# Expert order computed inside the first half of expert 0; three weights of expert 1 loaded and two split there; an own buffer for the places

## The chip, the core and the metric

The kernel runs on one core of a Trainium2 chip. Its time is the device time of one execution in microseconds (us), taken as the median of several executions; lower is better. TensorE (PE in the profile) has a granted clock with two levels, 1.2 and 2.4 GHz, which the profile writes as 0.50 and 1.00.

## The reference, cut to what matters

Three stages follow one another. Shapes: 4 batches, 8 heads, 768 positions, head size 48, so 3072 tokens of 384 values.

```python
for t in range(S):                                   # 1. linear attention with a decay
    state = alpha[:, :, t, :, None] * state + k_t v_t^T
    y[:, :, t] = q_t @ state
expert_idx = argmax(xn @ en.T / tau)                 # 2. each token goes to one of 8 experts
for e in range(8):
    out[mask_e] = gate_w[mask_e] * (relu(x[mask_e] @ w1[e]) @ w2[e])
for e in range(4):                                   # 3. every token through 4 experts
    out += p[:, e:e+1] * (relu(x @ w1[e]) @ w2[e])
```

Every expert has w1 of 384 x 1024 and w2 of 1024 x 384.

## The kernel before, in words

Stage 1 walks over 24 units of 128 tokens (loop `for i in range(NU + 5)` in `attention_and_routing`); unit u passes through `S1`, `S2` and `S3` in three successive rounds. Routing runs behind it in six groups of units: `route_a` picks each token's expert, `rank` counts the place within it on TensorE, `route_b` and `route_c` make the gate, `scale` applies it, and `scatter` writes the token's row (tile `xb`) with an indirect DMA of GpSimd into the region of its expert in `xs` in HBM.

Stage 2 runs the experts in the order of their number of tokens, expert 0 first and the others by falling count. Its windows have 448, 448, 432 ... 384 columns (`WIN`). Products are split for precision: each float32 operand becomes a rounded high part and a rest, and every product takes three matmuls. `h_split` cuts a hidden block so: ScalarE writes the high part `hh` with Relu, VectorE the rest `hl`. A weight unit (128 x 768, 384 KB; eight to an expert, units 0 to 7 are expert 0's, 8 to 15 those of the next) is loaded by `load_w` through SP's queue into one of 3 buffers `wraw`, and split by `split_w` into one of 10 buffers `wu`: ScalarE copies the high part (L74), GpSimd subtracts (L75).

The first 224 columns of expert 0 (`EARLY`) are done while stage 1 ends: `early_load` reads their rows, `early_rows` turns them over on TensorE and cuts them, `early_g1(f)` is the first product of block f, `early_relu(b)` cuts blocks 2b and 2b+1 (its rest, the "rest" of the change's name, is a VectorE instruction), `early_g2(f)` the second product. The function `tail` sets their order. At its end, between `early_g1(7)` and `early_g2(4)`, the matmul `pc` adds up the tokens of each expert. VectorE then computes from `pc` the order of the experts `ordi` (L938 to L945), the columns `offi`, and through the tile `pv` the place of each token, `posi` (L948 to L963).

Then `experts` starts. `window(e)` loads the rows of an expert with SP's queue (L173) into one of two buffers `xw`; for expert 0 these are the remaining 224 columns, in three pieces. `place(e)` (L203) reads `ordi` into an SP register, which the loads of expert 1 and later, rows and weights, have in their addresses. `xpose(e)` turns a window over on TensorE, and ScalarE (L197) and VectorE (L198) cut it; `columns` writes finished columns into `x2` (L218, L219). The loop over e and f issues for each block first product, `h_split`, and the second product `g2` of the block before. `xpose(1)` is spread over blocks 3 and 4 of expert 0 and the start of expert 1.

Every engine, SP's queue too, works in the order in which the program issues: the instruction order is written out by hand, and a wait of one instruction holds all behind it on its engine. The buffers of stage 2 lie in memory that the pools of stage 1 gave back; the first writer of such a buffer waits for the last reader of what lay there.

Of the kernel before, what the change touches and what calls it, by code (L numbers as in the profile page):

```python
# [20 lines left out]
NFB = FF // 128  # L21
# [92 lines left out]
def experts(ctx, tc, a, keep, small, xs, info_d, scat, wtile, ids, load_w, split_w, out, banks, psA, ps1):  # L114
# [8 lines left out]
    def h_split(ps, n):  # L123
        hh = hp.tile([128, 512], F32R, tag="hh", name="hh")
        hl = hp.tile([128, 512], F32R, tag="hl", name="hl")
        nc.scalar.activation(out=hh[:, 0:n], in_=ps, func=AF.Relu)  # L126
        nc.vector.scalar_tensor_tensor(  # L127
            out=hl[:, 0:n], in0=ps, scalar=0.0, in1=hh[:, 0:n].bitcast(F32), op0=ALU.max, op1=ALU.subtract
        )
        return hh, hl  # L130
# [23 lines left out]
    with ExitStack() as c1:  # L154
# [52 lines left out]

        window(0)
        place(1)
        load_w(NFB + 1)  # L210
        window(1)
        regs = {}
        xpose(0)
        pos, hs = {}, {}
# [25 lines left out]
        for e in range(E1):  # L240
            if e == 1:

                xpose(1, [2])
                g2(*prev)
                prev = None
                banks.close()
                psx = c1.enter_context(tc.tile_pool(name="psx", bufs=2, space=PSUM, reuse_waits="tile"))
                psh = c1.enter_context(tc.tile_pool(name="psh", bufs=3, space=PSUM, reuse_waits="tile"))
                pso = c1.enter_context(tc.tile_pool(name="pso", bufs=1, space=PSUM, reuse_waits="tile"))
                bank["h"] = lambda: psh.tile([128, W0], F32, tag="h", name="h")  # L250
                bank["xt"] = lambda e, k: psx.tile([128, W0], F32, tag="xt", name="xt")
                bank["o"] = lambda d: pso.tile([128, W0], F32, tag=f"o{d}", name=f"o{d}")
            for f in range(NFB):
                if e or f > 1:
                    split_w(e * NFB + f + 9)
                if f == 1 and e + 2 < E1:
                    place(e + 2)
                    window(e + 2)
                n = SIZE[e]
                ps = bank["h"]()[:, 0:n]  # L260
                xh, xl = xts[e]
                gemm1(ps, wtile[e * NFB + f], lambda k: xh[:, k, 0:n], lambda k: xl[:, k, 0:n])
                hs[e, f] = h_split(ps, n)
                if prev:
                    g2(*prev)
                prev = (e, f)
                if 3 <= f < (6 if e else 5) and e + 1 < E1:
                    xpose(e + 1, [f - 3])
                if e == 1 and f == 2:
                    pfl = bank["h"]()[0:1, 0:1]  # L270
                    nc.tensor.matmul(pfl, lhsT=keep["ft"][:, 0:1], rhs=keep["ones"][:, 0:1], start=True, stop=True)
                    nc.vector.tensor_copy(keep["flag"], pfl)
                if e and f == 2:
                    regs[e] = column(nc.scalar, e), column(nc.vector, e)
                if f % 2 and 4 <= e * 4 + f // 2 < 28:
                    info(e * 4 + f // 2 - 4)
            if e == E1 - 1:
                ins = nc.sync.dma_start(out=infc, in_=info_d.rearrange("(t p) c -> p t c", p=128))
                after(ins, infs, "all rows")
                nc.vector.tensor_scalar(toki, infc[:, :, 4], float(NT - 1), 0.0, op0=ALU.min, op1=ALU.max)  # L280
# [58 lines left out]
def attention_and_routing(tc, a, small, keep, xs, info_d, wst, wtile, load_w, split_w, psA, ps1):  # L339
# [5 lines left out]
    with ExitStack() as ctx:  # L345
# [464 lines left out]

        def tail(hl0):
            hl0()
            hl1 = early_relu(1)
            hl1()
            early_g2(0)
            early_g2(1)
            early_g1(4)
            early_g1(5)
            hl2 = early_relu(2)
            hl2()  # L820
            early_g2(2)
            early_g2(3)
            early_g1(6)
            early_g1(7)
            hl3 = early_relu(3)
            hl3()
            pc = er["pc"] = mk("pc", 128, 8)
            nc.tensor.matmul(pc, lhsT=oneb, rhs=cum, start=True, stop=True)
            for f in range(4, NFB):
                early_g2(f)  # L830

        for i in range(NU + 5):
            for g in range(2, NG):
                if max(0, 3 * g - 8) == i:
                    load_in(g, 0)
                if max(0, 3 * g - 6) == i:
                    load_in(g, 1)
            for g in range(1, NG):
                if 3 * g - 2 == i:
                    load_v(g)  # L840
            if 0 < i <= E1:
                prefill(i - 1)
            if 5 <= i < 27 and i % 2:
                load_w(min((i - 3) // 2, NFB))

            steps = []
            for g in range(1, NG):
                for pp in range(2):
                    at = 3 * g - 4 + pp - (g > 2)
                    if g == 1 and pp == i:  # L850
                        steps.append((2, lambda g=g, pp=pp: prep1(g, pp)))
                    if g > 1 and at + 1 == i:
                        steps.append((0, lambda g=g, pp=pp: prep1(g, pp, part=1)))
                    if g > 1 and at == i:
                        steps.append((1, lambda g=g, pp=pp: prep1(g, pp, part=0)))
            steps = [f for _, f in sorted(steps, key=lambda x: x[0])]
            if steps and i > 1:
                steps.pop(0)()
            if 0 < i < NU:
                S1(i)  # L860
            if i == 1:
                prep_emb3()
            if 0 <= i - 2 < NU:
                S3(i - 2)
            for r, (u0, u1) in enumerate(groups):
                if i == u1 + 2 and r < last:
                    rank(r)
            if 0 <= i - 1 < NU:
                S2(i - 1)
            for r, (u0, u1) in enumerate(groups):  # L870
                if i == u1 + (3 if r < last else 2) and r <= last:
                    route_b(r)
                if i == u1 + 1:
                    flush(sums)
                    if r > last:
                        early_g1(0)
                    route_a(r)
                    if r >= last:
                        rank(r)
                    if r > last:  # L880
                        early_g1(1)
                        hl0 = early_relu(0)
                        early_g1(2)
                        early_g1(3)
            for f in steps:
                f()
            for g in range(1, NG):
                for pp in range(2):
                    at = 3 * g - 3 + pp - (g > 2)
                    if at == i:  # L890
                        prep2(g, pp, nc.gpsimd, nc.gpsimd)
                    if at + 1 == i:
                        prep4(g, pp)
            if i == 0:
                fill()
            if i == 2:
                prep_info()
            for r, (u0, u1) in enumerate(groups):
                if i == u1 + 1 and r > last:
                    route_b(r)  # L900
                if i == u1 + (4 if r < last else 2 if r == last else 1):
                    route_c(r)
                    scale(r)
                    if r < last:
                        scatter(r)
                    if r > last:
                        scatter(last)
                        scatter(r)
                        count(r)
                        tail(hl0)  # L910
            if 6 <= i < 22 and i % 2 == 0:
                split_w((i - 4) // 2)
            flush(late)
            flush(sums)
            if i == EARLY_U + 5:
                early_load()
            if i == NU:
                early_rows()
        cnt, key, num, srt, offc = (
            c1.tile([128, 8], F32, name=n) for n in ("cnt", "keys", "num", "srt", "offc")  # L920
        )
# [22 lines left out]
        dot(srt, sel, iot)  # L944
        nc.vector.tensor_scalar(keep["ordi"], srt, float(E1 - 1), 0.0, op0=ALU.min, op1=ALU.max)  # L945

        dot(srt, sel, cnt)
        nc.vector.tensor_tensor(out=num, in0=srt, in1=wins, op=ALU.min)  # L948
        nc.vector.tensor_tensor_scan(offc[:, 1:8], ones[:, 1:8], num[:, 0:7], 0.0, op0=ALU.mult, op1=ALU.add)
# [3 lines left out]

        dot(off, gt3, cnt)
        nc.vector.tensor_tensor(out=off, in0=off, in1=loff[:, 1, :], op=ALU.subtract)
        pv = wk.tile([128, NU, 8], F32, tag="At", name="pv")
        nc.vector.tensor_tensor(
            out=pv, in0=ohb, in1=off.unsqueeze(1).to_broadcast([128, NU, 8]), op=ALU.mult
        )
# [1 line left out]
        nc.vector.tensor_reduce(out=pf, in_=pv, op=ALU.add, axis=AX.X)  # L961
        nc.vector.tensor_tensor(out=pf, in0=pf, in1=slotf, op=ALU.add)
        nc.vector.tensor_scalar(keep["posi"], pf, float(NT - 1), 0.0, op0=ALU.min, op1=ALU.max)  # L963

        ft = keep["ft"]
        nc.vector.tensor_reduce(out=ft[0:R, 0:1], in_=aacc, op=ALU.max, axis=AX.XY)
# [330 lines left out]
```

## Time and profile before

| | |
|---|---|
| time, median of 3 runs | 1237.86 us (1236.94 to 1239.62) |
| time of the profiled execution | 1224.77 us |
| its span, first to last instruction | 1222.9 us |
| mean granted TensorE clock | 0.982 |
| busy: PE, PEld, DVE, ACT, POOL | 1179.8, 1082.2, 394.3, 331.3, 306.6 us |
| HBM traffic | 64 GB/s over the span |

PE is TensorE's matmuls, PEld its weight loads, DVE VectorE, ACT ScalarE, POOL GpSimd, SP the engine that issues most loads. The times of the views below are us from the span's start. Stage 1 lies at 0 to about 159 us, the early half of expert 0 at 159 to 181, its other half at 181 to 212, the other experts of stage 2 until about 400, stage 3 after that.

### The profile page before, as it was taken

How to read it: one execution, taken by the hardware profiler on the slowest of the kernel's cores; microseconds unless marked ns; L12 is line 12 of the kernel's file. 1: busy time of each engine (PE TensorE's matmuls, PEld its weight loads, DVE VectorE, ACT ScalarE, POOL GpSimd, SP SyncE). 2: the span in 40 equal slices, each digit the busy share in tenths (PEclk: the TensorE clock that was granted, in tenths of full speed). 3: DMA queues.
4: the chain of work that ended last, by engine and by line, in shares of the span. 5: the costliest groups of instructions: out<-in, count | busy, mean ns of one | idle time of the engine just before them, and what ended most of it. 6: DMA issues, size and time to landing. Idle time of an engine off the chain costs nothing.

```text
span 1222.9 us, 17442 instructions
## 1 busy us (share of the span) xinstructions
PE 1179.8 (96%) x7219; PEld 1082.2 (88%) x7219; DVE 394.3 (32%) x823; ACT 331.3 (27%) x640; POOL 306.6 (25%) x221
## 2 busy tenths in 40 slices
PE   5899988999999999999999999999999999999996
PEld 4788887999999999999999999999999999999996
DVE  7999652223322222222122222222222122222221
ACT  2466624444444311111311111221111131111111
POOL 3468624666676300000400000130000030111111
PEclk9899987999999999999999999999999999999998
DMA  9996216544433300000200000020000010000000
GB/s 218 275 287 207 74 64 185 149 133 133 141 117 118 93 1 1 1 1 1 78 26 1 1 1 1 26 79 1 1 1 1 1 40 1 27 27 26 26 27 29
DMA packets 30032, 79.98 MB, mean 65 GB/s; under 512 B 7352, under 2 KB 11064, under 8 KB 28376
## 3 DMA queue, kind: packets, MB, share of 16 engines
q1 hardware_dynamic: 26104, 69.25, 19.8%
q0 software_dynamic: 3840, 9.54, 2.2%
q8 instruction: 58, 0.95, 0.3%
q14 instruction: 30, 0.25, 0.1%
HBM read 65.21 MB, written 13.57 MB: 64 GB/s over the span
## 4 chain that ended last, share of the span: by engine, by line
PE 85%; DVE 4%; issue 3%; DMA 1%; POOL 1%; SPq 0%; ACT 0%; DVEq 0%; POOLq 0%; ACTq 0%
PE h L135 13%; PE h L137 13%; PE h L136 13%; PE p L303 10%; PE p L302 10%; PE p L301 10%; PE o L232 3%; PE o L233 3%; PE o L234 3%; DVE bf L446 1%; PE eh L702 1%; DVE At L485 1%; DVE G L434 1%; DMA wraw<-in_wu_dram 1%; PE A L480 1%
## 5 line engine op out<-in xcount | busy, mean ns | idle before, releaser
L127 DVE SCALAR_TENSOR_TENSOR hl<-h,hh 128x512 fp32r<-128x512 f32 (+9 forms) x264 | 169.9, 644 | 742.5 <-ACT hh L126 742.5
L75 POOL TENSOR_TENSOR wu<-wraw,wu 128x768 fp32r<-128x768 f32 x96 | 176.7, 1842 | 653.6 <-ACT wu L74 653.4
L126 ACT ACTIVATE hh<-h 128x512 fp32r<-128x512 f32 (+9 forms) x264 | 147.6, 559 | 668.1 <-PE h L137 668.1
L303 PE MATMUL p<-wu,hl 128*128 128x384 f32 x768 | 259.0, 337 | 0.0
L302 PE MATMUL p<-wu,hh 128*128 128x384 f32 x768 | 258.4, 336 | 0.0
L301 PE MATMUL p<-wu,hh 128*128 128x384 f32 x768 | 258.2, 336 | 0.0
L135 PE MATMUL h<-x,wu 128*128 128x512 f32 (+1 forms) x600 | 233.1, 388 | 0.0
L137 PE MATMUL h<-x,wu 128*128 128x512 f32 (+1 forms) x600 | 230.7, 385 | 0.0
L136 PE MATMUL h<-x,wu 128*128 128x512 f32 (+1 forms) x600 | 228.1, 380 | 0.0
L302 PEld LDWEIGHTS p<-wu,hh 128*128 128x128 f32 x768 | 144.4, 188 | 7.4
L301 PEld LDWEIGHTS p<-wu,hh 128*128 128x128 f32 x768 | 144.5, 188 | 7.1
L303 PEld LDWEIGHTS p<-wu,hl 128*128 128x128 f32 x768 | 144.4, 188 | 0.0
L137 PEld LDWEIGHTS h<-x,wu 128*128 128x128 f32 x600 | 112.6, 188 | 26.5
L136 PEld LDWEIGHTS h<-x,wu 128*128 128x128 f32 x600 | 112.9, 188 | 16.0
L135 PEld LDWEIGHTS h<-x,wu 128*128 128x128 f32 x600 | 112.9, 188 | 14.5
L74 ACT ACTIVATE wu<-wraw 128x768 fp32r<-128x768 f32 x96 | 80.8, 843 | 85.1 <-PE o L234 37.0
L232 PE MATMUL o<-hh,wu 128*128 128x224 f32 (+7 forms) x192 | 66.5, 346 | 3.5 <-ACT hh L126 3.5
L314 POOL DMA_INDIRECT out_dram<-acc,toki x24 | 23.4, 974 | 183.4 <-DVE acc L310 178.5
L135 PE MATMUL h<-xh,wu 128*128 128x224 f32 (+7 forms) x192 | 68.8, 358 | 0.5 <-DVE xl L198 0.5
L136 PE MATMUL h<-xh,wu 128*128 128x224 f32 (+7 forms) x192 | 66.8, 348 | 0.0
L137 PE MATMUL h<-xl,wu 128*128 128x224 f32 (+7 forms) x192 | 66.7, 347 | 0.0
L233 PE MATMUL o<-hl,wu 128*128 128x224 f32 (+7 forms) x192 | 66.3, 345 | 0.0
(164 smaller groups left out, 1092.0 us busy)
## 6 DMA issues: line engine op xcount, KB each, us to landing
wraw<-in_wu_dram SPq DMA_DIRECT2D x96, 384.0 KB, 3.1
tin<-in_aqk_dram SPq DMA_DIRECT2D x14, 1011.1 KB, 12.0
xw<-xs SPq DMA_DIRECT2D x7, 672.0 KB, 6.3
v<-in_v_dram SPq DMA_DIRECT2D x8, 576.0 KB, 9.4
xs<-pre SPq DMA_DIRECT2D x8, 480.0 KB, 11.8
tin<-in_aqk_dram SPq DMA_DIRECT2D x2, 448.0 KB, 8.6
tin<-in_aqk_dram SPq DMA_DIRECT2D x2, 225.8 KB, 5.7
tin<-in_aqk_dram SPq DMA_DIRECT2D x2, 224.0 KB, 3.4
```

What stands on the lines that cost most here:

```text
L74: nc.scalar.activation(out=t[:, 0], in_=r, func=AF.Copy)
L75: nc.gpsimd.tensor_tensor(out=t[:, 1], in0=r, in1=t[:, 0].bitcast(F32), op=ALU.subtract)
L126: nc.scalar.activation(out=hh[:, 0:n], in_=ps, func=AF.Relu)
L127: nc.vector.scalar_tensor_tensor(out=hl[:, 0:n], in0=ps, scalar=0.0, in1=hh[:, 0:n].bitcast(F32), op0=ALU.max, op1=ALU.subtract)
L135: nc.tensor.matmul(ps, lhsT=w[:, 0, ks], rhs=xh(k), start=(k == 0), stop=False)
L136: nc.tensor.matmul(ps, lhsT=w[:, 1, ks], rhs=xh(k), start=False, stop=False)
L137: nc.tensor.matmul(ps, lhsT=w[:, 0, ks], rhs=xl(k), start=False, stop=(k == KD - 1))
L232: nc.tensor.matmul(o, lhsT=w[:, 0, ds], rhs=hh[:, 0:n], start=(f == 0), stop=False)
L233: nc.tensor.matmul(o, lhsT=w[:, 0, ds], rhs=hl[:, 0:n], start=False, stop=False)
L301: nc.tensor.matmul(o, lhsT=hh[:, js], rhs=w[:, 0, DM:2 * DM], start=(f == 0), stop=False)
L302: nc.tensor.matmul(o, lhsT=hh[:, js], rhs=w[:, 1, DM:2 * DM], start=False, stop=False)
L303: nc.tensor.matmul(o, lhsT=hl[:, js], rhs=w[:, 0, DM:2 * DM], start=False, stop=(f == NFB - 1))
```

## The change

`pc` moves from the end of `tail` to behind `early_g2(1)`, and the instructions that compute `ordi` follow directly. The early products of blocks 4 to 7 and their cuts are issued behind that, and the last cut `early_relu(3)` behind `posi`. `pv` gets a buffer of its own in the pool of constants instead of a turn in the buffers `At`. `early_rows` moves behind `S3(23)` and the last `route_a`. Of expert 1, units 8, 9 and 10 are loaded ahead of its window (one unit before), and units 8 and 9 are split ahead of `xpose(0)`. In the loop a unit is split behind `h_split` instead of ahead of the first product, with a lead of 6 blocks that grows to 9 (9 throughout before).

```diff
@@ experts
         window(0)
         place(1)
-        load_w(NFB + 1)
+        load_w(NFB + 3)
         window(1)
+        split_w(NFB + 2)
         regs = {}
         xpose(0)
...
             for f in range(NFB):
-                if e or f > 1:
-                    split_w(e * NFB + f + 9)
...
                 hs[e, f] = h_split(ps, n)
+                split_w(e * NFB + f + min(9, 6 + max(0, e * NFB + f - NFB) // 3))
                 if prev:
                     g2(*prev)
@@ attention_and_routing, tail
-            hl1 = early_relu(1)
-            hl1()
+            early_relu(1)()
             early_g2(0)
             early_g2(1)
-            early_g1(4)
-            early_g1(5)
-            hl2 = early_relu(2)
-            hl2()
-            early_g2(2)
-            early_g2(3)
-            early_g1(6)
-            early_g1(7)
-            hl3 = early_relu(3)
-            hl3()
             pc = er["pc"] = mk("pc", 128, 8)
             nc.tensor.matmul(pc, lhsT=oneb, rhs=cum, start=True, stop=True)
-            for f in range(4, NFB):
-                early_g2(f)
@@ the loop over units
                 if i == u1 + 1:
                     flush(sums)
+                    route_a(r)
                     if r > last:
-                        early_g1(0)
-                    route_a(r)
+                        early_rows()
                     if r >= last:
                         rank(r)
                     if r > last:
+                        early_g1(0)
                         early_g1(1)
...
-            if i == NU:
-                early_rows()
@@ behind the loop
         nc.vector.tensor_scalar(keep["ordi"], srt, float(E1 - 1), 0.0, op0=ALU.min, op1=ALU.max)
+        early_g1(4)
+        early_g1(5)
+        early_relu(2)()
+        early_g2(2)
+        early_g2(3)
+        early_g1(6)
+        early_g1(7)
         dot(srt, sel, cnt)
...
-        pv = wk.tile([128, NU, 8], F32, tag="At", name="pv")
+        pv = c1.tile([128, NU, 8], F32, name="pv")
...
         nc.vector.tensor_scalar(keep["posi"], pf, float(NT - 1), 0.0, op0=ALU.min, op1=ALU.max)
+        early_relu(3)()
+        for f in range(4, NFB):
+            early_g2(f)
```

## Rows read from the trace of the kernel before

**Rows 1.** The profile's first page, busy time of each engine.

```profile
PE 1179.8 (96%) x7219; PEld 1082.2 (88%) x7219; DVE 394.3 (32%) x823; ACT 331.3 (27%) x640; POOL 306.6 (25%) x221
```

**Rows 2.** What TensorE waited for, 159 to 400 us: total, times, longest (us).

```profile
PE xt L192 <- DMA xw<-xs: 4.2, 2, 3.9
PE o L232 <- ACT hh L126: 3.5, 1, 3.5
PE ext L686 <- DMA exw<-xs: 1.8, 1, 1.8
```

**Rows 3.** The same view, 214 us to the end.

```profile
PE h L135 <- DVE xl L198: 0.3, 1, 0.3
```

**Rows 4.** Stretches: length; busy us (instructions) of PE, PEld, DVE, ACT, POOL; clock, DMA share, GB/s.

```profile
150.80:152.50 1.70, 0.00 (x1) 0.01 (x1) 1.39 (x9) 0.14 (x2) 1.40 (x2) 1.00 0.43 162
154.10:157.40 3.30, 3.30 (x32) 2.55 (x27) 1.81 (x12) 0.88 (x4) 0.94 (x2) 0.50 0.31 82
161.20:167.70 6.50, 6.48 (x32) 6.37 (x33) 3.98 (x23) 1.48 (x5) 3.72 (x4) 0.50 0.34 124
...
181.20:185.10 3.90, 0.03 (x1) 0.00 (x0) 2.43 (x14) 0.00 (x0) 0.00 (x0) 0.96 0.14 41
185.10:187.50 2.40, 1.83 (x6) 0.87 (x6) 0.78 (x2) 0.89 (x3) 0.00 (x0) 0.50 0.49 112
...
195.60:199.20 3.60, 0.17 (x2) 0.00 (x0) 0.00 (x0) 1.95 (x4) 1.19 (x1) 0.90 0.39 121
199.20:205.20 6.00, 5.96 (x27) 5.82 (x28) 1.80 (x4) 2.60 (x5) 5.54 (x4) 0.50 0.53 147
206.28:212.15 5.87, 5.87 (x54) 5.87 (x54) 1.80 (x4) 3.94 (x7) 4.48 (x3) 1.00 0.47 138
212.30:214.00 1.70, 1.42 (x15) 1.24 (x12) 0.69 (x2) 1.26 (x4) 0.82 (x1) 1.00 0.78 219
```

**Rows 5.** What SP's queue waited for, 150 to 400 us: total, times, longest.

```profile
SPq L173 <- DVE pf L961: 11.7, 1, 11.7
```

**Rows 6.** Line L173, the window loads: durations (ns), time to landing (us).

```profile
L173 SPq EVENT_SEMAPHORE  x7: 17/28/10652, 166.4 to 187.6; - x7
...
DMA to landing us min/median/max: 2.5/6.1/8.5
```

**Rows 7.** Instructions in order of time, 150 to 185 us.

```profile
158.25 1.62 ACT L645 ACTIVATE xb<-xb,gt 128x384 f32<-128x384 f32 x3
...
159.96 0.79 ACT L675 ACTIVATE ext<-ext 128x448 fp32r<-128x448 f32 x2
...
160.98 0.20 ACT L563 ACTIVATE lt<-fin 128x32 f32<-128x32 f32 x1 [0.23 <-PE fin L558]
...
161.54 0.49 ACT L570 ACTIVATE xb<-fin 128x384 f32<-128x384 f32 x1
...
168.69 2.38 PE L724 MATMUL eo<-eh,wu 128*128 128x224 f32 x18
...
177.71 0.63 DVE L711 SCALAR_TENSOR_TENSOR eh<-eh 128x448 fp32r<-128x448 f32 x1 [3.34 <-ACT eh L710]
178.26 0.15 DVE L938 COPY cnt<-rkb 128x8 f32<-128x8 f32 x1
...
179.93 0.17 DVE L945 TENSOR_SCALAR ordi<-srt 128x8 int32<-128x8 f32 x1
...
182.13 0.35 DVE L961 TENSOR_REDUCE pf<-pv 128x24 f32<-128x192 f32 x1
...
182.55 1.94 SPq L173 DMA_DIRECT2D xw<-xs  x3
```

**Rows 8.** The same view, 185 to 235 us.

```profile
185.89 0.37 SPq L64 DMA_DIRECT2D wraw<-in_wu_dram  x1
...
197.09 0.84 ACT L74 ACTIVATE wu<-wraw 128x768 fp32r<-128x768 f32 x1 [4.23 <-DMA wraw<-in_wu_dram]
```

**Rows 9.** Line L64, the weight loads: time to landing (us).

```profile
DMA to landing us min/median/max: 2.8/3.1/12.3
```

## Prediction

> **What bounds the kernel now.** I read the first page, then TensorE's waits, then the stretches in which it waits, then what was late there. TensorE is busy for 1179.8 us, 96% of the span; no other engine passes 32% [rows 1]. From 214 us to the end it waits only 0.3 us [rows 3], so from there on the order of the weights can win next to nothing, and what is won ahead of 214 us moves the end one for one. The change acts between 157 and 214 us. There TensorE waits 4.2 us for the rest of expert 0's window (transposes L192) and 3.5 us for ScalarE's `hh` [rows 2].
>
> The stretches show what each wait costs beyond itself [rows 4]. From 181.2 to 185.1 TensorE stands still (0.03 us busy), and the next stretch has clock 0.50, the 1.2 GHz level. From 195.6 to 199.2 it stands still again, and the 6 us behind that run at 0.50: 27 matmuls in 6.00 us, where 54 take 5.87 us at 1.00. So 0.22 us a matmul against 0.109: six microseconds at half clock lose three.
>
> What is late? The window load was issued at 182.55; its queue waited 11.7 us for the instruction L961, which reads `pv` [rows 5]. `pv` has nothing to do with the window: it lies in memory that the window's buffer takes over. The longest semaphore wait of that line is 10.65 us [rows 6], so everything else (the scattered rows) was there at 182.55 - 10.65 = 171.9. L961 itself is late because its chain hangs on `pc`, which stands behind `early_g1(7)`: VectorE copies `cnt` at 178.26, writes `ordi` at 179.93 and runs L961 at 182.13 [rows 7]. The second wait: ScalarE's copy of unit 9 stands ahead of `hh` of block 2 and waits 4.23 us for its weights until 197.09 [rows 8]; that load was issued behind the windows of experts 1 and 2.
>
> **The parts, one by one.** I write X for the time at which TensorE ends the early products: 181.2 before.
>
> *`early_rows` behind `S3(23)`.* ScalarE's three pieces of S3 (160.98 to 162.03, 1.05 us) now stand ahead of the two cuts that start at 159.96 [rows 7]. The scaling from 158.25, 1.62 us, ends at 159.87 either way. So the cuts, and `early_g1(0)` behind them, start about 1.1 us later. In return `rank`, which stood between the early products, is done in the gap. The stretch up to 167.7 has half clock [rows 4], so 1.1 us there is some 5 matmuls, 0.55 us at full clock. Bounds 0 and 1.1; I take 0.3, since the rank matmuls and their wait leave that path. X is 181.5.
>
> *`pc` and `ordi` earlier.* `early_g2(0)` and `(1)` run from 168.69 for 2.38 us [rows 7]; with 0.3 us of delay `pc` ends at 171.5. From `cnt` to the end of `ordi` it took 180.10 - 178.26 = 1.84 us, and 0.1 us lies ahead, so `ordi` is there at 173.4 instead of 180.1. On VectorE this stands ahead of the rest of blocks 4 and 5, and the 2.9 us from `ordi` to `posi` ahead of the rest of blocks 6 and 7, 0.63 us [rows 7]. Blocks 4 and 5 leave TensorE at about 173.6, so their rest ends by 174.8; `posi` ends by 177.8, the last rest by 178.7. `early_g2(6)` reads it at X - 2 = 179.5. Cost nothing, covered by 0.8 us.
>
> *`pv` alone.* The window load no longer waits for L961. It is issued when the last scattered rows have landed, 171.9 plus 0.3 us, and its three issues take 1.94 us [rows 7]. The longest landing of that line, 8.5 us [rows 6], would be 182.5; a third of a window should lie at its minimum, 2.5 us, so about 176.5. The transposes then follow the early products without a gap.
>
> *Loads and splits.* From the first window issue at 182.55 to unit 8's issue at 185.89 it was 3.34 us [rows 7, 8]. So units 8, 9 and 10 go out at about 175.5, 176.1 and 176.7, the window of expert 1 behind them. At the median landing of 3.1 us [rows 9] units 8 and 9 are there at 178.6 and 179.2. ScalarE copies them (0.84 us each, [rows 8]) until 180.2. Queued behind on ScalarE are the copies of `xpose(0)`, the first due at X + 0.4 = 181.9, then `columns` and `hh` of block 0. Cost nothing, covered by 1.7 us; without the cover every microsecond is one on TensorE's path. GpSimd's two subtractions fall in a stretch in which it is idle (the stretch from 181.2, [rows 4]). The copies that waited until 197.09 are gone from the loop: unit 10 comes at block 5, long loaded. The smaller lead (6 blocks) is 12 us of first-half blocks; a load needs 3.1 us, 12.3 at worst [rows 9]. I put it at nothing.
>
> *The second half itself.* Before: from 181.2 to 212.15, where expert 1's last transposes begin, 30.95 us. After: the transposes and cuts ahead of the first product took 2.40 us at half clock with a wait for the window's second piece in it (the stretch from 185.1, [rows 4]); without, VectorE and ScalarE set a floor of about 1.4 us; I take 2.0. Then 15 groups of nine matmuls: 54 took 5.87 us, so 15 x 0.98 = 14.7 us. Eight transposes, 0.15 us each at most (half of 1.83 / 6), less what overlaps: 0.8 us. And `g2(0)` will wait for `hl` of block 0, which stands behind three `columns` cuts on ScalarE (0.3 us each) and VectorE (0.39 us each, both from the row at 185.1): 0 to 0.9 us, taken as 0.6. Sum 18.1 us.
>
> **The clock.** This sum holds clock 1.00. The gap around `xpose(0)` shrinks from 3.9 us to pieces of 0.7 and 0.6 us. The rows have a case on either side [rows 4]: behind 1.7 us of standstill from 150.8 the clock was 0.50 from 154.1; around 212.3, with 0.28 us idle, it stayed 1.00. Idle pieces of 1.3 us in all lie between; I take 1.00, because they are split, and keep the loss as a rival. The Trainium skill ("TensorE: Matmul & The Clock Gate", "What's actually happening") says that the throttled state is the default and that activity releases it: it speaks against counting on full clock through a stretch of small transposes and waits. By that rule the sum would be 1.7 to 3 us worse; by the row at 212.3 it stands.
>
> **Sum.** 30.95 - 18.1 = 12.85 us, less 0.3 us for the later X: 12.5 us. The profiled execution goes from 1224.8 to 1212.3 us (span 1222.9 to 1210.4). It lies 13.1 us below the median of the runs shown; I take the same difference from the median: 1237.9 - 12.5 = 1225.4 us. A measurement here tells changes above about 0.2%, 2.5 us.
>
> **Rivals.**
> - *The clock falls in the transposes of expert 0.* One or two stretches at half clock, as behind 199.2 (6 us, 3 lost). Saving 9.5 to 10.8 us, 1227 to 1228.4. For it the row at 150.8, against it the split gaps.
> - *The early half also holds full clock.* With S3 and `early_rows` closer, the 6.5 us at 0.50 up to 167.7 could go: up to 3.2 us more, 1222.2. Against it: a gap before `rank` remains.
> - *ScalarE blocks on units 8 and 9.* They come late, `xpose(0)` stands behind their copies. If unit 9 needs 8.5 us, like a window, 3.7 us are lost: 1229. This is also the case that ends slower: the whole gain is gone when unit 9 lands 12.5 us past the 181.05 at which its copy is still in time, at 193.5, that is 17.4 us after its issue. The longest weight load in the trace took 12.3 us [rows 9]. Against it: ahead of unit 9 stand only unit 8 and a third of a megabyte of expert 0's window, while the load that ended at 197.09 stood behind two whole windows.
> - *The change does not free the window.* Another late reader, such as the early products in the shared memory, holds the load until X. Then the 3.9 us and the half clock behind them (3 us) stay, and only the wait for unit 9 with its half clock goes: 5.5 us, 1232.4. Against it: the wait of 10.65 us was the last of its line.
>
> **How the numbers follow.** My forecast 0.54 (1223.5 to 1227); clock falls 0.20; early half at full clock 0.07; ScalarE late but still faster 0.10; window not freed 0.05; ScalarE so late that nothing is won or time is lost 0.04. The range from the early half at full clock with some rest (1221.5) to ScalarE late by 6 us (1231.5) leaves out about 0.1. Faster by over 0.2%: 0.94; within: 0.02; slower: 0.04.
>
> **What would show it.** In the profile after: `ordi` near 173.4; the window's issue near 172 to 174, no longer released by L961; the first weight issue near 175.5; no wait of L192 for its window and none of L232 for `hh` above 1 us; the first transposes of expert 0 near 181.5 and expert 1's last near 199.6; clock 1.00 from 168 on. Wrong would be: a wait of the copies L197 behind L74, a 0.50 behind 181, a window issue past 177, or new waits behind 200 where the split's lead is shorter.

## The result and the profile after

| | before | after |
|---|---|---|
| median of 4 runs each | 1237.4 us (1236.2 to 1239.6) | 1224.2 us (1219.3 to 1226.7) |
| ratio, 95% interval | | 0.9886 [0.9852, 0.9920] |
| span of the profiled execution | 1222.9 us | 1217.5 us |

The change takes 13.2 us off the median, 1.1%. The two profiled executions lie only 5.4 us apart; why is told below, and it is not the change. The first page of the profile after, its span and the busy time of each engine:

```profile
span 1217.5 us, 17436 instructions
...
PE 1177.6 (97%) x7219; PEld 1078.6 (89%) x7219; DVE 393.9 (32%) x823; ACT 326.5 (27%) x640; POOL 306.8 (25%) x221
```

TensorE is busy for 2.2 us less than in [rows 1], with the same 7219 matmuls: fewer of them run at half clock (mean granted clock 0.987 against 0.982). What TensorE waited for from 150 to 400 us (total, times, longest, us):

```profile
PE U L537 <- issue: 2.7, 3, 1.1
PE rkb L592 <- DVE ohb L1012: 1.3, 1, 1.3
...
PE xt L192 <- DVE xl L198: 0.7, 1, 0.7
PE h L135 <- DVE xl L198: 0.3, 1, 0.3
PE eh L702 <- DVE ext L676: 0.2, 1, 0.2
```

The two long waits of [rows 2], 4.2 us for the window and 3.5 us for `hh`, are gone. The largest one that is left belongs to stage 1 (L537, "issue": TensorE waited for nothing that the profile shows). The stretches (length; busy us and instructions of PE, PEld, DVE, ACT, POOL; clock, DMA share, GB/s):

```profile
171.60:175.20 3.60, 3.60 (x20) 3.60 (x20) 1.88 (x11) 0.65 (x2) 1.46 (x2) 0.53 0.31 114
176.20:188.70 12.50, 12.43 (x112) 12.23 (x111) 7.16 (x32) 3.34 (x5) 3.12 (x3) 1.00 0.52 175
188.70:190.20 1.50, 0.82 (x8) 0.51 (x6) 0.69 (x2) 0.60 (x2) 1.50 (x2) 1.00 0.79 209
190.20:206.74 16.54, 16.39 (x145) 16.18 (x144) 5.67 (x14) 6.98 (x17) 3.79 (x3) 1.00 0.36 107
```

The reader should hold this against [rows 4]. Half clock is left in the first products of the early half (171.6 to 175.2, 0.53). From 176.2 on the clock is 1.00 and stays there: through the end of the early half at 188.7, through the transposes (1.5 us) and through the second half up to 206.74. What SP's queue waited for at the window loads, 150 to 400 us:

```profile
SPq L173 <- DMA xs<-xb,si: 14.6, 3, 12.6
```

[rows 5] had L961, VectorE's read of `pv`, in that place; now it is the scattered rows. Instructions in order of time (lines behind 200 are shifted by a few against the kernel before; L955 is the old L961):

```profile
178.51 0.18 PE L817 MATMUL rkb<-cum,oneb 128*128 128x8 bf16 x1
...
178.73 0.17 DVE L924 COPY cnt<-rkb 128x8 f32<-128x8 f32 x1 [1.14 <-PE rkb L817]
...
179.52 1.94 SPq L173 DMA_DIRECT2D xw<-xs  x3
...
180.42 0.17 DVE L931 TENSOR_SCALAR ordi<-srt 128x8 int32<-128x8 f32 x1
...
182.84 1.54 SPq L64 DMA_DIRECT2D wraw<-in_wu_dram  x3
...
185.98 0.85 ACT L74 ACTIVATE wu<-wraw 128x768 fp32r<-128x768 f32 x1 [0.58 <-DMA wraw<-in_wu_dram]
...
187.33 0.85 ACT L74 ACTIVATE wu<-wraw 128x768 fp32r<-128x768 f32 x1 [0.50 <-DMA wraw<-in_wu_dram]
...
188.68 0.55 PE L192 MATMUL xt<-ti,xw 112*128 112x112 f32 x4
```

`pc` at 178.51, `ordi` at 180.42, the window's loads at 179.52, the three weights from 182.84, their copies on ScalarE (L74) at 185.98 and 187.33, and the first transposes at 188.68, directly behind the early products.

To compare executions I use three instants that the view in order of time gives for each kernel: the end of stage 1 (last matmul of L525), X (last matmul of `early_g2`) and T (start of expert 1's last transposes, the last four of L192 ahead of expert 1's first product):

| | end of stage 1 | X | T | X to T | T to the end |
|---|---|---|---|---|---|
| before | 157.45 | 181.24 | 212.15 | 30.91 | 1010.7 |
| after | 166.08 | 188.84 | 206.74 | 17.90 | 1010.8 |

From T on the two executions agree within 0.1 us. From X to T 13.0 us are won, from the end of stage 1 to T 14.0 us (54.70 against 40.66); this second stretch is called the hand-over below, and its part up to X the early half. Stage 1, which the change leaves as it is, took 8.6 us longer in the execution profiled after: 14.0 - 8.6 = 5.4, the difference of the spans.

### The profile page after: what moved, and what is told of

It is laid out like the page before. It is cut to its first block, busy times and chain, and to the rows that moved or that the text cites. A ratio compares the mean times of both kernels' runs of the same rounds, so it can differ in the third digit from the quotient of the medians.

```text
span 1217.5 us, 17436 instructions
## 1 busy us (share of the span) xinstructions
PE 1177.6 (97%) x7219; PEld 1078.6 (89%) x7219; DVE 393.9 (32%) x823; ACT 326.5 (27%) x640; POOL 306.8 (25%) x221
## 4 chain that ended last, share of the span: by engine, by line
PE 87%; DVE 4%; issue 3%; ACT 0%; POOL 0%; DVEq 0%; POOLq 0%; ACTq 0%
PE h L135 14%; PE h L137 13%; PE h L136 13%; PE p L303 11%; PE p L302 11%; PE p L301 10%; PE o L234 3%; PE o L235 3%; PE o L233 3%; PE fin L558 1%; PE y L516 1%; PE A L480 1%; DVE bf L446 1%; DVE G L434 1%; DVE At L485 1%
## 5 line engine op out<-in xcount | busy, mean ns | idle before, releaser
L136 PEld LDWEIGHTS h<-x,wu 128*128 128x128 f32 x600 | 112.8, 188 | 16.1
L74 ACT ACTIVATE wu<-wraw 128x768 fp32r<-128x768 f32 x96 | 80.4, 840 | 39.6 <-PE p L303 34.1
L314 POOL DMA_INDIRECT out_dram<-acc,toki x24 | 23.4, 975 | 183.4 <-DVE acc L310 178.5
L135 PE MATMUL h<-xh,wu 128*128 128x224 f32 (+7 forms) x192 | 67.4, 351 | 0.3 <-DVE xl L198 0.3
L136 PE MATMUL h<-xh,wu 128*128 128x224 f32 (+7 forms) x192 | 65.5, 341 | 0.0
```

The lines of the kernel that those rows point to most:

```text
L74: nc.scalar.activation(out=t[:, 0], in_=r, func=AF.Copy)
L135: nc.tensor.matmul(ps, lhsT=w[:, 0, ks], rhs=xh(k), start=(k == 0), stop=False)
L136: nc.tensor.matmul(ps, lhsT=w[:, 1, ks], rhs=xh(k), start=False, stop=False)
```

## The experiments

All twelve runs, with X to T from the profile of each and the ratio to the kernel before on the same chip:

| run | X to T, us | ratio [95% interval] |
|---|---|---|
| before, again | 29.71 | 1.0014 [0.9992, 1.0035] |
| after, again | 17.90 | 0.9871 [0.9846, 0.9895] |
| after, `pv` shared | 24.04 | 0.9931 [0.9904, 0.9959] |
| after, weights as before | 19.66 | 0.9896 [0.9863, 0.9928] |
| before, own `pv` alone | 25.80 | 0.9945 [0.9914, 0.9976] |
| own `pv` and weights, order as before | 25.31 | 0.9954 [0.9930, 0.9978] |
| after, `early_rows` as before | 17.91 | 0.9882 [0.9842, 0.9922] |
| after, window ahead of the weights | 20.12 | 0.9924 [0.9895, 0.9953] |
| after, with fillers | 20.52 | 0.9904 [0.9881, 0.9926] |
| after, third piece in its own bank | 18.65 | 0.9893 [0.9853, 0.9934] |
| order alone | 24.56 | 0.9953 [0.9927, 0.9978] |
| weights alone | 29.36 | 0.9980 [0.9958, 1.0002] |

From T to the end every one of them took 1010.7 to 1010.8 us, with the shorter lead of the splits and without it, so the lead, which the prediction put at nothing, cost nothing there.

**Before, again.** No edit.

> The kernel before, unchanged, in a new profile. Two stretches are compared in all runs: stage 1, up to the last matmul of S2 of unit 23 (157.4 us in the profile before, 166.1 after), and the hand-over, from there to the first of expert 1's last transposes (54.7 us before, 40.7 after). My theory: the hand-over is a property of the order and repeats within 1.5 us (54 to 56 us here), and stage 1 varies by several us from one execution to the next, so that the profile before was a short one (this one 160 to 172 us). Rival: the change itself lengthens stage 1 (through code or memory that moved), and stage 1 is again 157 to 158 here.

Hand-over 54.74 us against 54.70. Stage 1 ended at 151.92, so the profile before was not a short one, as I had put it; but it does vary without any change of the kernel, which the rival denied. TensorE's waits from 145 to 235 us are those of [rows 2] in other sizes, and a wait of the early second products (L724) for VectorE that the first profile does not have:

```profile
PE xt L192 <- DMA xw<-xs: 4.0, 1, 4.0
PE ext L686 <- DMA exw<-xs: 2.9, 1, 2.9
PE o L232 <- ACT hh L126: 2.5, 1, 2.5
...
PE eo L724 <- DVE eh L711: 1.6, 1, 1.6
```

**After, again.** No edit.

> The changed kernel, unchanged, in a new profile and five rounds. My theory: hand-over 40 to 42 us again, stage 1 anywhere between 157 and 170, time about 13 us below before (ratio 0.988 to 0.991). Rival (the change lengthens stage 1): stage 1 again at 165 to 167 us.

1209.9 us against 1224.0 for before on this chip, 14.1 us where about 13 were expected. X to T is 17.90 us once more. Stage 1 ended at 155.04, so the change does not lengthen it. The hand-over was 43.35 us, a miss against the expected 40 to 42: the early half took 25.45 us here, 22.76 in the first profile. Two waits in it were not there in the first profile:

```profile
PE ext L686 <- DMA exw<-xs: 1.3, 1, 1.3
PE eo L724 <- DVE eh L711: 0.9, 1, 0.9
```

The early half thus varies between executions of the same kernel, by 2.7 us here, while X to T did not vary in the two profiles of after and varied by 1.2 us in those of before. X to T is the better measure of the change: 13.0 us from before to after, 11.8 us in this second pair of profiles.

**After, `pv` shared.**

```diff
-        pv = c1.tile([128, NU, 8], F32, name="pv")
+        pv = wk.tile([128, NU, 8], F32, tag="At", name="pv")
```

> The changed kernel with pv back in the buffers At, all else as after. My theory: the window load waits for the read of pv again, which the earlier order puts some 4 us ahead of the end of the early products; the reading of ordi and the weights stand behind it in SP's queue, units 8 and 9 come 4 to 5 us later, ScalarE's copies hold the transposes of expert 0: hand-over 44.5 to 48 us, 4 to 7 us slower than after. Rival (the earlier order alone is enough, the buffer is idle): 40 to 42 us, the same time as after.

Hand-over 47.99 us, as my theory had it at its upper end. Instructions in order of time:

```profile
183.20 0.35 DVE L955 TENSOR_REDUCE pf<-pv 128x24 f32<-128x192 f32 x1
...
183.63 1.94 SPq L173 DMA_DIRECT2D xw<-xs  x3
...
186.96 1.55 SPq L64 DMA_DIRECT2D wraw<-in_wu_dram  x3
...
187.77 0.55 PE L192 MATMUL xt<-ti,xw 112*128 112x112 f32 x4
...
190.16 0.84 ACT L74 ACTIVATE wu<-wraw 128x768 fp32r<-128x768 f32 x1 [5.67 <-DMA wraw<-in_wu_dram]
...
192.41 0.84 ACT L74 ACTIVATE wu<-wraw 128x768 fp32r<-128x768 f32 x1 [1.40 <-DMA wraw<-in_wu_dram]
193.16 0.58 ACT L197 ACTIVATE xh<-xt 128x224 fp32r<-128x224 f32 x2
```

The window load starts 0.08 us behind the end of the read of `pv` (183.20 + 0.35), 5 us later than after measured from X. The window itself still comes in time: the first transposes run at 187.77. But the weights stand behind it in the queue (186.96), ScalarE copies them until 193.25, and only then cuts the first transposed piece (193.16, 5.4 us behind the start of the transposes; after: 0.4 us).

**After, weights as before.**

```diff
-        load_w(NFB + 3)
+        load_w(NFB + 1)
         window(1)
-        split_w(NFB + 2)
...
+                if e or f > 1:
+                    split_w(e * NFB + f + 9)
...
-                split_w(e * NFB + f + min(9, 6 + max(0, e * NFB + f - NFB) // 3))
```

> The changed kernel with the weights part undone: one unit ahead of the window, no split ahead of the transposes, splits in the loop ahead of the first product with a lead of 9. Order and buffer as after. My theory: the window comes in time, but ScalarE waits in block 2 for unit 9, whose load stands behind the window of expert 2, 3 to 5 us, and the clock falls behind it (2 to 3 us): hand-over 45 to 49 us. Rival (with ordi early the loads are early enough by themselves): 40 to 42 us.

Hand-over 44.14 us, X to T 19.66: a miss. Only 1.8 us are lost, because the wait for `hh` is much shorter than the 3.5 us of [rows 2], and the clock stays at 1.00 behind it. The wait, and the stretch behind it (columns as in [rows 4]):

```profile
PE o L232 <- ACT hh L126: 0.9, 1, 0.9
```

```profile
190.70:200.37 9.67, 9.67 (x88) 9.51 (x87) 2.82 (x6) 5.66 (x11) 8.86 (x5) 1.00 0.61 181
```

The window of expert 1 went out 5.4 us ahead of X here, some 5 us behind it before. Unit 9, still issued behind the windows, landed 4.9 us after its issue instead of 8.7.

**Before, own `pv` alone.** The buffer line above in the kernel before.

> The kernel before with one edit, the own buffer for pv. My theory: the window of expert 0 is loaded some 10 us earlier and the 3.9 us wait with most of its half clock goes, the wait for unit 9 stays, since ordi and the loads behind it are as late as before: hand-over 47 to 50 us against 54.7, time 5 to 7 us below before. Rival (the window is held by something else too): 54 to 55.5 us, the time of before.

Hand-over 48.70 us and 7.0 us off the time, as expected (X to T accounts for 4.5 us of the time; the interval of the ratio is 3.0 to 10.6 us). The wait for the window is gone; what is left, and a part new, is:

```profile
PE xt L192 <- DVE xl L198: 2.8, 1, 2.8
PE o L232 <- ACT hh L126: 2.4, 1, 2.4
```

VectorE's instructions in order of time:

```profile
194.99 0.16 DVE L972 TENSOR_REDUCE ft<-fl 128x1 f32<-128x4 f32 x1
195.16 0.69 DVE L198 TENSOR_TENSOR xl<-xt,xh 128x224 fp32r<-128x224 f32 x2
```

The first wait is new: with the order as before, VectorE is busy with the chain behind `pc` until 195.15 and cuts the first piece only then, 2.76 us behind X (192.40). The early order thus frees VectorE too, not only SP's queue.

**Own `pv` and weights, order as before.** The kernel before with the buffer line and the weights part of the change.

> The kernel before with the own buffer and the weights part, but pc and ordi behind early_g1(7) as before and early_rows at its old place. My theory: units 8 and 9 are issued only behind ordi, 6 to 7 us later than after, ScalarE's copies of them hold the transposes of expert 0 by 4 to 5 us and the clock falls: hand-over 46 to 50 us, so the early order is worth 5 to 9 us. Rival (the early order is idle once buffer and weights are right): 40.5 to 42.5 us.

Hand-over 48.21 us. The transposes are held for 6.6 us, since the third piece waits for the cut of the first, and that for ScalarE's copies of units 8 and 9:

```profile
PE xt L192 <- DVE xl L198: 6.6, 1, 6.6
```

**After, `early_rows` as before.**

```diff
                 if i == u1 + 1:
                     flush(sums)
-                    route_a(r)
                     if r > last:
-                        early_rows()
+                        early_g1(0)
+                    route_a(r)
                     if r >= last:
                         rank(r)
                     if r > last:
-                        early_g1(0)
...
+            if i == NU:
+                early_rows()
```

> The changed kernel with early_rows back at the end of the round before, ahead of S3 of unit 23, and early_g1(0) ahead of route_a. My theory: worth next to nothing, hand-over within 1.5 us of after (40 to 42 us), same time. Rival (the move keeps TensorE busier and the clock up in the early half): 42.5 to 45 us.

Hand-over 40.39 us, early half 22.48 against 22.76: this part of the change is worth nothing that shows. The first early product starts 3.40 us behind the end of stage 1 instead of 4.35, but the early half does not get shorter by that.

**After, window ahead of the weights.**

```diff
-        load_w(NFB + 3)
         window(1)
+        load_w(NFB + 3)
```

> The changed kernel with the window of expert 1 (672 KB) ahead of the three weight loads in SP's queue instead of behind them. My theory: units 8 and 9 land 2 to 4 us later, the 1.7 us of cover are used up and ScalarE's copies hold the transposes of expert 0 by 1 to 3 us: hand-over 41.5 to 45 us. Rival (the loads share the DMA engines, so their order hardly matters): 40 to 41.5 us.

X to T 20.12, hand-over 42.83 us. The same loads in another order cost 2.2 us. One wait grows from the 0.7 us of after to 1.8 us, and the clock, 1.00 there in after, falls behind it: 23 matmuls take 4.00 us, which at the 0.109 us of a matmul at full clock [rows 4] would be 2.5 us. The wait, and the stretch behind it:

```profile
PE xt L192 <- DVE xl L198: 1.8, 1, 1.8
```

```profile
195.60:199.60 4.00, 4.00 (x23) 3.98 (x23) 1.99 (x6) 1.35 (x5) 1.06 (x1) 0.57 0.85 228
```

**Order alone, and weights alone.** The changed kernel with both other parts undone, and the kernel before with the weights part only.

> The changed kernel with the weights part and the buffer part undone: only the earlier pc and ordi and the moved early_rows are left. Theory: the window load waits for the read of pv, some 4.3 us ahead of the end of the early products, and just comes in time; the wait for unit 9 stays, and longer than in the run that had the own buffer: from the end of the early products to expert 1's last transposes 21 to 25 us (before 29.7 to 30.9, after 17.9), so this part alone brings more than half. Rival: without the buffer the order brings under 3 us.

> The kernel before with the weights part alone: three units loaded ahead of the window of expert 1, two split ahead of the transposes, splits in the loop behind h_split; pc, ordi, early_rows and pv as before. Theory: units 8 and 9 go out some 5 us behind the end of the early products and ScalarE's copies of them hold the transposes by 5 to 6 us more, which eats what the missing wait in block 2 gives back: 28 to 32 us from the end of the early products to expert 1's last transposes, time within 2 us of before. Rival: the missing wait is worth more than the later transposes: 24 to 26 us.

The order alone gives 24.56 us, in the stated range; but that is 5.7 us below before (mean of its two profiles 30.3), a little under half of the 12.4 us of the whole change, where more than half was expected. One long wait of TensorE is left:

```profile
PE o L232 <- ACT hh L126: 4.1, 1, 4.1
```

The weights alone give 29.36 us, as expected; the median is 2.4 us below before, just past the expected 2 us, and the interval of the ratio includes no gain. The transposes wait first for the window and then for ScalarE:

```profile
PE xt L192 <- DVE xl L198: 6.6, 1, 6.6
PE xt L192 <- DMA xw<-xs: 4.2, 2, 3.9
```

**Fillers.**

```diff
+        def spin(n):
+            for _ in range(n):
+                nc.tensor.matmul(dcon[:, 0:128], lhsT=oneb[:, 0:R], rhs=trib, start=True, stop=True)
...
+            if i == NU + 1:
+                spin(10)
...
+                        spin(16)
                         early_rows()
+                        spin(14)
                     if r >= last:
                         rank(r)
                     if r > last:
+                        spin(3)
                         early_g1(0)
```

> The changed kernel with 43 filler matmuls (bfloat16, 128 columns, into a PSUM bank that is free by then) in the gaps of TensorE between the last matmul of S2 and the first early product: 10 ahead of S3 of unit 23, 16 ahead of early_rows, 14 behind it, 3 behind rank. They compute nothing that is used. Question: what is left of the early half, 22.5 to 25.5 us in the runs so far, of which some 6 us run at clock 0.50. Theory: the standstills of about 3 us in all send the clock down, and with them filled it stays at 1.00: early half 1.5 to 3 us shorter (20.5 to 23), time 2 to 3 us below after. Rival: the gaps are too small a part, or the fillers stand in the way of the real work: early half the same or up to 1 us longer.

The theory fell. The fillers did keep the clock at 1.00 through the first products,

```profile
183.90:188.30 4.40, 4.37 (x37) 4.21 (x37) 3.17 (x18) 0.70 (x3) 1.25 (x3) 1.00 0.24 89
```

where after had 0.53 from 171.60 to 175.20, and the first products took 4.4 us instead of 5.9. But the early half lasted 23.37 us, 0.6 longer than after, and the ratio (0.9904; after, on other chips, 0.9886 and 0.9871) shows no gain either. The first products started 5.75 us behind the end of stage 1 (183.93 - 178.18), 1.4 us later than after (170.43 - 166.08), and the second products then waited for VectorE:

```profile
PE xt L192 <- DVE xl L198: 2.3, 1, 2.3
PE eh L702 <- DVE ext L676: 1.2, 1, 1.2
PE eo L724 <- DVE eh L711: 0.9, 1, 0.9
```

The 1.5 us that the clock gave are about the 1.4 us of the later start, and VectorE's waits come on top; whether a filling without a later start would gain stays open. The 2.3 us of L192 lie behind X and do not belong to the early half: there unit 9 came late, as in the next experiment.

**Third piece in its own bank.**

```diff
-            "xt": lambda e, k: psA.tile([128, W0], F32, tag="A", name="xt0") if e == 0
+            "xt": lambda e, k: psA.tile([128, W0], F32, tag="A", name="xt0") if e == 0 and k < 2
...
-        columns(keep["early"], slice(0, EARLY), slice(0, EARLY))
...
                 hs[e, f] = h_split(ps, n)
+                if e == f == 0:
+                    columns(keep["early"], slice(0, EARLY), slice(0, EARLY))
```

> The changed kernel with the third transposed piece of expert 0's window in a PSUM bank of its own instead of that of the first piece, and the early columns written behind the first h_split instead of ahead of it. Theory: the wait of 0.68 us of the third piece for VectorE goes, and the second product no longer waits for the rest of block 0: from the end of the early products to expert 1's last transposes 16.8 to 17.5 us against 17.9. Rival: ScalarE and VectorE set the pace there whatever the bank: 17.8 to 18.2.

Inconclusive: X to T 18.65 us, outside both ranges. The six transposes of 199.19 do run in one go now, but unit 9 landed late in this execution, ScalarE waited 2.21 us for it and began the cuts at 200.35, 1.2 us behind the start of the transposes instead of 0.4:

```profile
199.19 0.74 PE L192 MATMUL xt<-ti,xw 112*128 112x112 f32 x6
199.60 0.84 ACT L74 ACTIVATE wu<-wraw 128x768 fp32r<-128x768 f32 x1 [2.21 <-DMA wraw<-in_wu_dram]
...
200.35 0.83 ACT L197 ACTIVATE xh<-xt 128x224 fp32r<-128x224 f32 x3
```

## Why the prediction was right

The forecast was 1225.4 us from 1237.9, a gain of 12.5 us; the runs give 13.2 us [9.9 to 18.3 by the interval of the ratio], and 14.1 us on the second chip.

*The window.* Right. The issue was put 9.3 us ahead of X and came 9.32 us ahead (188.84 - 179.52), released by the scattered rows. The prediction named `pv` alone as what held it. The runs say it more exactly: the early order alone also brings the window in time (first transposes directly behind X, with `pv` shared), and so does the buffer alone. Each is enough for the window; both are needed for what stands behind the window in SP's queue, and the early order for VectorE, which otherwise cuts the first piece late.

*`ordi` and the weights.* The forecast had `ordi` 8.1 us and the first weight issue 6.0 us ahead of X; they came 8.25 us (180.42 + 0.17) and 6.00 us ahead. The cover of the splits was mis-sized: put at 1.7 us, it measured 0.9 (unit 9's copy ends at 188.18, the first cut starts at 189.07), and 0.8 to 1.0 in the profiles of after, after again and `early_rows` as before. The term at fault is the landing of unit 9: forecast at the median, 3.1 us after its issue, and there only after 3.9. With fillers and with the third bank, unit 9 was there only 6.4 and 5.6 us after its issue, and X to T was 2.6 and 0.8 us longer. Both ran on one chip, on which the changed kernel itself was not profiled: whether the chip, the edit or the execution made unit 9 late stays open. The rival "ScalarE blocks on units 8 and 9" is thus close by. Put wholly into it, by shared `pv`, order as before or weights alone (there with the wait for the window), X to T is 24.0, 25.3 and 29.4 us.

*The weights part.* Mis-sized as a share. The prediction let the wait for `hh` and its half clock, 3.5 and 3 us, go because of the loads and splits. Undoing that part alone loses 1.8 us, since with `ordi` early and an own `pv` that wait is 0.9 us even with the old loads; with `ordi` early and `pv` shared (order alone) it is 4.1 us. What shortens it is thus in the main that SP's queue is free early. Which of the part's three edits (more loads ahead, splits ahead of the transposes, splits behind `h_split`) gives the 1.8 us was not taken apart. Parts alone against the mean of the two profiles of before (30.3): order 5.7, buffer 4.5, weights 0.9; all three 12.4.

*The second half.* 18.1 us forecast from X to T, 17.90 measured, twice. That it is so close is in part luck: from X to the first product it took 1.36 us (188.84 to 190.20) instead of 2.0, from there to T 16.54 us instead of 16.1, and the two errors cancel.

*The clock.* 1.00 from 176.2 on, as the row at 212.3 in [rows 4] had it; the gap around the transposes did not bring it down in either profile of the changed kernel. The loss that the prediction feared from the sentence on the throttled default (the Trainium skill, "TensorE: Matmul & The Clock Gate", "What's actually happening") did not come. But the margin is small: where the wait of the third piece grew from 0.7 us to 1.8 (window ahead of the weights) or 2.3 us (fillers), the clock fell behind it, to 0.57 from 195.60 to 199.60 and 0.56 from 204.90 to 208.40. So the rival "the clock falls in the transposes" came true in these two runs. With the third bank, where TensorE waited 1.2 us for VectorE ahead of the first product, the clock stayed at 1.00.

*`early_rows`.* Put at 0.3 us of loss. Early half 23.79 before and 22.76 after in one pair, 25.03 and 25.45 in the other, 22.48 with the old place: no effect beyond how executions differ. Among the nine profiles with the longer stage 1 (last section) the early half is 22.5 to 22.9 us with either order, 23.4 with the fillers. The rival that it would lift the clock in the early half is out: 0.53 is still there. The fillers lifted it and won nothing, but they also made the first products start later.

*The base.* The prediction took the 13.1 us between the profile before and its runs as a constant. For the median that came out; for the profiled execution it did not: 1212.3 us was forecast and 1219.3 measured, 4.9 us below its own median, because its stage 1 was 8.6 us longer than that of the profile before. That the 13.1 us lie in stage 1 is inferred: no execution of the kernel before near 1237.9 us was profiled, but the two profiles of after differ by 8.4 us up to X and by less than 0.1 us from X to T and from T to the end. Had the 13.1 us lain in the hand-over, the sum could have been wrong. The rows ahead of the prediction could not tell, so in this point it had luck.

## What to carry to other kernels

Find what a load really waits for by the longest semaphore wait of its line: here it was a VectorE scratch tile whose memory the load's buffer had inherited, and one line moved it. Order, buffer and weights act on one SP queue, the order on VectorE too, so the buffer and the order, worth 6.1 and 7.4 us on top of the other two parts, were worth 4.5 and 5.7 alone, and the weights, which looked like a 6 us gain, were worth 1 to 2. Work moved ahead of a critical step needs a cover measured from its slowest load, not the median: 1.7 us of forecast cover were 0.9, and gone in two of the later runs. A lost cover can cost twice: 1.1 us of further waiting brought 1.5 us of half clock behind it.

## What the runs showed that was not expected

Stage 1 of the same program ends at quite different times: 151.9 to 164.0 us in five profiles (before, before again, after again, shared `pv`, weights as before), 166.1 to 178.2 in the other nine. In the first five TensorE has not one "issue" wait up to 200 us; in the nine it has 12 to 17, 7.0 to 8.4 us in all, between the small matmuls of stage 1. These waits are only about half of the difference: the five end stage 1 at 156.9 us in the mean, the nine at 172.0. TensorE's waits up to 175 us of the run with the order as before (total, times, longest, us):

```profile
PE U L537 <- issue: 3.1, 4, 1.1
...
PE A L480 <- issue: 2.7, 6, 0.9
...
PE fin L558 <- issue: 1.3, 2, 0.8
...
PE rkb L592 <- issue: 0.5, 1, 0.5
PE kn L492 <- issue: 0.3, 1, 0.3
```

The kernel before took 1224.0 us on the chip of the first four experiments, 1236.7 and 1237.7 us on the chips of the others, while from T to the end all profiles agree within 0.15 us. So the profile before, at 1224.8 us, was of the one kind, and the runs shown with it, at 1237.9, probably of the other, of which the profile after is one; what holds TensorE's instructions back there was not tried.
